# Loads of v and stores of x cut at other partitions in a talking-heads attention kernel

## The chip, the cores and the metric

The kernel runs on one core of one Trainium2 chip. The metric is the time of one execution on the device in microseconds (us). The kernel before takes 866.6 us, the median of three runs that lie between 863.59 and 868.46 us.

## What is computed

Four batches of attention with 12 heads, 448 positions and a head size of 64, with heads mixed before and after the softmax, and behind it a bilinear feed-forward layer. All inputs are float32. Cut to what matters:

```python
scores = scale * np.matmul(q, k.transpose(0, 1, 3, 2))
scores = np.einsum('bhij,hg->bgij', scores, w_pre)
attn = np.exp(scores - np.max(scores, axis=-1, keepdims=True))
attn = attn / (np.sum(attn, axis=-1, keepdims=True) + 1e-09)
attn = np.einsum('bhij,hg->bgij', attn, w_post)
out = np.matmul(attn, v)                       # [4, 12, 448, 64]
x = out.transpose(0, 2, 1, 3).reshape(1792, 768)
a, b = x @ w_a, x @ w_b                        # 768 x 1536 each
result = (a * b) @ w_out
```

## The kernel before

The attention fills roughly the first 350 us, the feed-forward layer the rest.

Positions are cut into chunks of 120, 120, 120 and 88 per batch, and each chunk into units of 20 positions (23 units a batch, 92 in all). The main loop takes one unit in each step `s`. On TensorE a step holds four pieces of work: `premix` of its unit (L345, tile `mp`), one `qk` (L281, tile `pst`, scores of one pair of heads for a later chunk), one `av` (L429, tile `xp`, attention times v for two heads of a group of six units that is finished) and `postmix` of the unit before (L391, tile `pp`).

Between `qk` and `premix` the scores are laid out anew: `gather` (L325, tile `sb<-s`) copies them from SBUF to SBUF with four transfers for each unit, issued by POOL. A unit's gathers are issued four steps ahead (`AH`) into tiles that rotate over five buffers.

All other transfers of this stage go through the queue of SP, which issues them in the order of the program: loads of q (L251) and k (L235), loads of v (`load_v`, L206 to L218), stores of x to a buffer in device memory (L439, `xd<-xs`), and two writes of 4 bytes in each step (L221, `paced`), which wait for a result of VectorE and so hold SP's queue to the pace of the computation. `plan_loads` chooses the step of each load of q, k and v by an estimate of what each step already carries; its estimates for v stand in a list `v_size`, which the change leaves alone.

Loads of q (from the chunk with number 3 on) and of k (from the second batch on) are already cut in two by partitions, at row 88 (`LOW`, `part`). `load_k` of the later batches puts its rows in a tile with two buffers (`kraw`), so that the load with number i + 2 waits until `order_k` (L242 to L244) has copied the load with number i away.

`load_v` brings the v of one batch in 14 pieces, 7 for each half of the heads. A half lies in a tile of 128 partitions by 6 heads by 4 by 64. Pieces 0 to 2 are partitions 0 to 63, two heads each; pieces 3 and 4 are partitions 64 to 111, three heads each; pieces 5 and 6 fill the rest. The first 8 pieces of the first batch are loaded before the main loop, the others from step 3 on, those of a later batch while the batch before is computed.

`av` fills the tile `xs` (128 partitions by 3 by up to 120 columns) twice for each group; its store is issued one step later (`later(..., 1)`). There are 32 stores of x: 24 of 180 KB and 8 of 132 KB, eight for each batch. They are read back after the attention stage (L523, `xhl<-xd`).

Of the kernel before, what the change touches and what calls it, by code (L numbers as in the profile page):

```python
# [22 lines left out]
def talking_heads_bilinear_kernel(  # L23
# [11 lines left out]
    nc = tc.nc  # L35
    B, _, G, S = k.shape
# [10 lines left out]
    R = 4  # L47
    P = S // R
    C = 64
    X = P - C  # L50
# [21 lines left out]
    V_PIECES = 14  # L72
    PACKET = 170
    LOW = 88
    OWN = 3
    SPREAD = 2
    RAW_AT = 74
# [8 lines left out]
    for b in range(B):  # L86
        t0 = 0
        while t0 < S:
            n = min(CHUNK, S - t0)
# [30 lines left out]
    xd = [dram.tile([128, KD, S], F32, name=f"xd{b}") for b in range(B)]  # L120
# [21 lines left out]
    def later(fn, n=3):  # L142
        todo_at.setdefault(now[0] + n, []).append(fn)
# [61 lines left out]
    def load_v(b, i):  # L205
        g, i = divmod(i, V_PIECES // 2)  # L206
        to, of = vt[b % 2][g], v[b, g]
        if i < 3:
            heads = slice(2 * i, 2 * i + 2)
            nc.sync.dma_start(out=to[:C, heads], in_=of[:C, heads])  # L210
        elif i < 5:
            heads = slice(3 * (i - 3), 3 * (i - 3) + 3)
            nc.sync.dma_start(out=to[C:P, heads, :R - 1], in_=of[C:, heads, :R - 1])
        elif i == 5:
            for j in range(R - 1):
                nc.sync.dma_start(out=to[P:, :, j], in_=of[C + Y * j:C + Y * j + Y, :, R - 1])
        else:
            nc.sync.dma_start(out=to[C:, :, R - 1], in_=of[:C, :, R - 1])  # L218
# [4 lines left out]
    def part(half):  # L223
        return slice(0, 128) if half is None else slice(LOW * half, LOW + (128 - LOW) * half)

# [191 lines left out]
    def av(a, p):  # L417
        b, u0, _ = groups[a]
        t0 = (u0 - b * NUB) * QU
        n = min(AVC, S - t0)  # L420
        g = p // 3
        if p % 3 == 0:
            xp = ps.tile([128, 512], F32, tag="m" if a == NA - 1 else "x", name="xp", bufs=3 if a == NA - 1 else 1)
            xps[g] = xp[:, :3 * AVC].rearrange("p (a t) -> p a t", a=3)
        xp = xps[g]
        for r in range(R):
            for e in range(2):
                h = 2 * p + e
                nc.tensor.matmul(  # L429
                    xp[64 * e:64 * e + 64, p % 3, :n],  # L430
                    lhsT=vt[b % 2][g][:, h % G, r],
                    rhs=ptt[a][:, r, h, :n],
                    start=(r == 0),
                    stop=(r == R - 1),
                )
        if p % 3 == 2:
            xs = x_p.tile([128, 3, AVC], F32, tag="xs", name="xs")
            nc.vector.tensor_copy(xs[:, :, :n], xp[:, :, :n])
            later(lambda: nc.sync.dma_start(out=xd[b][:, 3 * g:3 * g + 3, t0:t0 + n], in_=xs[:, :, :n]), 1)  # L439

    items, late, between, after, ready = {}, {}, {}, {}, {}
    starts = [u for u in range(NU) if units[u][1] == 0] + [NU]
# [2 lines left out]
    for c in range(1, NC):  # L445
        b, t0, _ = chunks[c]
# [11 lines left out]
    for a in range(NA):  # L458
        b, u0, n = groups[a]
        for p in range(H // 2):  # L460
            av_at[a, p] = u0 + n + (AV_AT if n == GU else AV_SHORT)[p]
            if a < NA - 1:
                items.setdefault(av_at[a, p], []).append((av, a, p))

    def plan_loads():
# [6 lines left out]
        def place(first, last, it, n, parts=(0,)):  # L472
            for x in parts:
                u = min(range(min(first, last), last + 1), key=lambda u: (busy[u], u if len(parts) > 1 else -u))
                busy[u] += n
                full = sum(1 for y in between.get(u, ()) if y[0] in (load_q, load_k, load_v))
                (after if full else between).setdefault(u, []).append(it + ((x,) if len(parts) > 1 else ()))
                first = u
# [23 lines left out]
        for b in range(1, B):  # L502
            first = max(av_at[per_b * (b - 2) + per_b - 1, H // 2 - 1] + 1 if b > 1 else 0, V_FIRST + V_PIECES - V_EARLY)
            for i in sorted(range(V_PIECES), key=lambda i: (i // 7, -v_size[i % 7])):
                place(first, av_at[per_b * b, i // 7 * 3] - V_LEAD, (load_v, b, i), v_size[i % 7])
# [346 lines left out]
    with tc.manual_schedule():  # L852
# [16 lines left out]
        for i in range(G):  # L869
            if i == 1:  # L870
                spread_q(0, 1, nc.vector)
                setup_w()
            if i + 4 < G:
                load_k(0, i + 4)
                order_k(0, i + 4, pool, pool)
            if i == 2:
                load_q(1, 0)
                load_q(1, 1)
                for j in range(V_EARLY):
                    load_v(0, j)  # L880
                load_q(2, 0)
            qk(0, i, 0)
# [15 lines left out]
        for s in range(NU + 2):  # L898
# [19 lines left out]
            for it in items.get(s, ()):  # L918
                if it[0] is qk:
                    it += (it[2] % OWN if s not in late else 1,)  # L920
                it[0](*it[1:])
# [15 lines left out]
        for p in range(6):  # L937
            av(NA - 1, p)
            if p == 2:
                for fn in split_all(2):  # L940
                    fn()
# [73 lines left out]
        for n in range(NP * 2):  # L1015
            i, r = divmod(n, R6)
# [59 lines left out]
```

## Time and profile before

| | |
|---|---|
| three runs | 863.59, 866.6, 868.46 us |
| the profiled execution | 864.87 us, of which its span 863.2 us |
| TensorE matmul busy | 838.9 us, 97% of the span |
| VectorE, ScalarE, POOL busy | 500.7, 414.1, 478.9 us |
| DMA packets | 105306, 165.90 MB |
| SP's queue (q1) and POOL's queue (q0) | 46.1% and 18.5% of the time of 16 DMA engines |
| granted TensorE clock, mean | 0.995 |

The busy time of TensorE says little about how near it is to its peak, since matmuls are pipelined and their ends are modelled. What tells more is the idle time of its own, its releasers, and the distance from one `premix` to the next, which is 3.45 us in a step that holds all four pieces of work.

### The profile page before, as it was taken

How to read it: one execution, taken by the hardware profiler on the slowest of the kernel's cores; microseconds unless marked ns; L12 is line 12 of the kernel's file. 1: busy time of each engine (PE TensorE's matmuls, PEld its weight loads, DVE VectorE, ACT ScalarE, POOL GpSimd, SP SyncE). 2: the span in 40 equal slices, each digit the busy share in tenths (PEclk: the TensorE clock that was granted, in tenths of full speed). 3: DMA queues.
4: the chain of work that ended last, by engine and by line, in shares of the span. 5: the costliest groups of instructions: out<-in, count | busy, mean ns of one | idle time of the engine just before them, and what ended most of it. 6: DMA issues, size and time to landing. Idle time of an engine off the chain costs nothing.

```text
span 863.2 us, 26217 instructions
## 1 busy us (share of the span) xinstructions
PE 838.9 (97%) x10612; PEld 675.4 (78%) x10612; DVE 500.7 (58%) x989; ACT 414.1 (48%) x864; POOL 478.9 (55%) x595
## 2 busy tenths in 40 slices
PE   7898999999999999999999999999999999999998
PEld 3455665666656656798999999999999998999997
DVE  4777778777787776455433433363446245655761
ACT  3676677677777777634323232322232145333330
POOL 6786777677767865026446533678657743222220
PEclk9999999999999999999999999999999999999999
DMA  7687777787979984764643634566565488655551
GB/s 195 176 197 181 190 191 204 181 201 190 201 169 203 217 200 110 218 203 163 190 145 134 217 134 158 185 222 247 198 221 193 156 314 301 214 209 190 205 198 65
DMA packets 105306, 165.90 MB, mean 192 GB/s; under 512 B 50014, under 2 KB 81114, under 8 KB 105186
## 3 DMA queue, kind: packets, MB, share of 16 engines
q1 hardware_dynamic: 76738, 126.11, 46.1%
q0 software_dynamic: 28448, 38.11, 18.5%
q8 instruction: 84, 1.38, 0.7%
q14 instruction: 36, 0.29, 0.1%
HBM read 84.16 MB, written 41.29 MB: 145 GB/s over the span
## 4 chain that ended last, share of the span: by engine, by line
PE 65%; DMA 10%; POOL 9%; issue 7%; DVE 5%; ACT 2%; SPq 1%; POOLq 0%; DVEq 0%; ACTq 0%
PE xp L429 8%; PE pp L391 7%; PE pst L281 7%; PE mp L345 6%; PE po L759 6%; PE po L760 6%; PE po L758 6%; PE pb L641 3%; PE pa L639 3%; PE pa L640 3%; PE pa L641 3%; PE pb L639 3%; PE pb L640 3%; DMA sb<-s 3%; DMA kraw<-in_k_dram 2%
## 5 line engine op out<-in xcount | busy, mean ns | idle before, releaser
L325 POOL DMA_DIRECT2D sb<-s x354 | 204.1, 588 | 66.2 <-PE mp L345 28.9
L358 ACT ACTIVATE a<-mp,nm 124x448 f32<-124x448 f32 x180 | 112.6, 631 | 57.8 <-DVE nm L355 57.7
L355 DVE TENSOR_REDUCE nm<-mp 124x1 f32<-124x448 f32 x180 | 104.2, 619 | 51.2 <-PE mp L345 48.5
L661 DVE TENSOR_TENSOR hf<-pb,sa 128x448 f32<-128x448 f32 x47 | 29.4, 625 | 170.0 <-PE pb L641 155.8
L429 PEld LDWEIGHTS xp<-pt,v 128*64 128x64 f32 x1536 | 74.1, 137 | 61.7 <-issue 44.7
L645 ACT COPY sa<-pa 128x448 f32<-128x448 f32 x47 | 25.0, 533 | 175.8 <-PE pa L641 175.8
L408 ACT COPY pt<-pp 128x480 f32<-128x480 f32 x176 | 91.2, 576 | 34.6 <-PE pp L391 33.5
L391 PE MATMUL pp<-kr,a 60*64 60x60 f32 x5040 | 99.3, 223 | 5.3 <-issue 4.9
L391 PEld LDWEIGHTS pp<-kr,a 60*64 60x64 f32 x5040 | 86.5, 135 | 21.9 <-issue 9.6
L641 PE MATMUL pb<-xhl,wl 128*128 128x448 f32 x282 | 102.4, 363 | 0.9 <-POOL wl L624 0.9
L639 PE MATMUL pb<-xhl,wh 128*128 128x448 f32 x282 | 102.3, 363 | 0.0
L640 PE MATMUL pb<-xhl,wh 128*128 128x448 f32 x282 | 102.3, 363 | 0.0
L281 PE MATMUL pst<-k,q 64*64 64x448 f32 (+1 forms) x728 | 92.5, 546 | 7.5 <-DVE s L306 4.4
L345 PE MATMUL mp<-sb,wp 60*64 60x448 f32 x720 | 96.2, 547 | 2.7 <-DMA sb<-s 1.8
L640 PE MATMUL pa<-xhl,wh 128*128 128x448 f32 x264 | 95.7, 363 | 0.0
L641 PE MATMUL pa<-xhl,wl 128*128 128x448 f32 x264 | 95.7, 363 | 0.0
L639 PE MATMUL pa<-xhl,wh 128*128 128x448 f32 x264 | 95.7, 363 | 0.0
L429 PE MATMUL xp<-pt,v 128*64 128x120 f32 (+1 forms) x1536 | 93.5, 266 | 0.8 <-ACT pt L408 0.8
L630 POOL TENSOR_TENSOR wl<-v,wh 128x768 fp32r<-128x768 f32 x21 | 39.2, 1868 | 98.9 <-ACT wh L629 96.4
L759 PE MATMUL po<-hhl,wh 128*128 128x448 f32 x252 | 91.6, 364 | 1.6 <-DVE hhl L717 1.6
L758 PE MATMUL po<-hhl,wh 128*128 128x448 f32 x252 | 91.4, 363 | 0.0
L760 PE MATMUL po<-hhl,wl 128*128 128x448 f32 x252 | 91.4, 363 | 0.0
(117 smaller groups left out, 1432.7 us busy)
## 6 DMA issues: line engine op xcount, KB each, us to landing
sb<-s POOLq DMA_DIRECT2D x350, 105.0 KB, 5.1
hhl<-hd SPq DMA_DIRECT2D x42, 448.0 KB
v<-in_w_ab_dram SPq DMA_DIRECT2D x22, 768.0 KB
hd<-hf SPq DMA_DIRECT2D x48, 224.0 KB
v<-in_w_out_dram SPq DMA_DIRECT2D x12, 768.0 KB
wod<-cw SPq DMA_DIRECT2D x21, 384.0 KB
v<-wod SPq DMA_DIRECT2D x21, 384.0 KB
xhl<-xd SPq DMA_DIRECT2D x24, 224.0 KB
```

What stands on the lines that cost most here:

```text
L281: nc.tensor.matmul(out[64 * e:64 * e + cols.stop - cols.start], lhsT=qt[c, i // QG][rows, i % QG, cols], rhs=kt[b, i][rows],)
L325: (nc.sync if ALONE <= u <= AH and i % 2 else nc.gpsimd).dma_start(out=sbt[u][i % 2][r:r + m * H], in_=rows)
L345: nc.tensor.matmul(mt[u, i // 2][col:col + M], lhsT=wp[r:r + m, :M], rhs=tiles[i % 2][r:r + m])
L358: nc.scalar.activation(a[:m], mp[:m], ACTF.Exp, bias=nm[:m], scale=1.0, accum_out=rss[u][:m, j:j + 1])
L391: nc.tensor.matmul(pp_t[i][C * e:C * e + C, H * r:H * r + H, j, :m], lhsT=at[u, j][rows, x:x + C], rhs=kr[rows, j, :, :m],)
L429: nc.tensor.matmul(xp[64 * e:64 * e + 64, p % 3, :n], lhsT=vt[b % 2][g][:, h % G, r], rhs=ptt[a][:, r, h, :n], start=(r == 0), stop=(r == ...
L639: nc.tensor.matmul(o, lhsT=hh[:, off + k], rhs=x[:, 0, k], start=first, stop=False)
L640: nc.tensor.matmul(o, lhsT=hh[:, off + k], rhs=x[:, 1, k], start=False, stop=False)
L641: nc.tensor.matmul(o, lhsT=ll[:, off + k], rhs=x[:, 0, k], start=False, stop=last)
L758: nc.tensor.matmul(po, lhsT=hh[:, k], rhs=t[:, 0, k], start=(k == 0), stop=False)
L759: nc.tensor.matmul(po, lhsT=hh[:, k], rhs=t[:, 1, k], start=False, stop=False)
L760: nc.tensor.matmul(po, lhsT=ll[:, k], rhs=t[:, 0, k], start=False, stop=(k == KH2 - 1))
```

## The change

Two things. In `load_v`, pieces 0 to 2 become partitions 0 to 23 with all six heads, and partitions 24 to 63 with three heads in each of two pieces; pieces 3 and 4 become partitions 64 to 87 and 88 to 111 with all six heads each. The number of pieces and their bytes in sum stay (600 KB for the five pieces of a half). In `av`, each store of x of the first three batches becomes two stores, of partitions 0 to 87 and 88 to 127, issued one behind the other in the step in which the one store was issued; the last batch keeps its eight stores whole.

```diff
+    C_LOW = 24
...
         if i < 3:
-            heads = slice(2 * i, 2 * i + 2)
-            nc.sync.dma_start(out=to[:C, heads], in_=of[:C, heads])
+            rows, heads = ((slice(0, C_LOW), slice(0, G)), (slice(C_LOW, C), slice(0, 3)), (slice(C_LOW, C), slice(3, G)))[i]
+            nc.sync.dma_start(out=to[rows, heads], in_=of[rows, heads])
         elif i < 5:
-            heads = slice(3 * (i - 3), 3 * (i - 3) + 3)
-            nc.sync.dma_start(out=to[C:P, heads, :R - 1], in_=of[C:, heads, :R - 1])
+            n = X // 2
+            rows = slice(C + n * (i - 3), C + n * (i - 3) + n)
+            nc.sync.dma_start(out=to[rows, :, :R - 1], in_=of[rows, :, :R - 1])
...
             nc.vector.tensor_copy(xs[:, :, :n], xp[:, :, :n])
-            later(lambda: nc.sync.dma_start(out=xd[b][:, 3 * g:3 * g + 3, t0:t0 + n], in_=xs[:, :, :n]), 1)
+            for half in range(2) if b < B - 1 else (None,):
+                rows = part(half)
+                later(lambda rows=rows: nc.sync.dma_start(out=xd[b][rows, 3 * g:3 * g + 3, t0:t0 + n], in_=xs[rows, :, :n]), 1)
```

## Rows read from the trace of the kernel before

**Rows 1.** The page, part 1: engine, busy us (share of the span), instructions.

```profile
PE 838.9 (97%) x10612; PEld 675.4 (78%) x10612; DVE 500.7 (58%) x989; ACT 414.1 (48%) x864; POOL 478.9 (55%) x595
```

**Rows 2.** Busy us (instructions) of each engine by stretch, then clock, DMA share, GB/s.

```profile
57.00:72.00 15.00, 11.85 (x305) 7.19 (x303) 10.52 (x32) 8.85 (x21) 10.65 (x19) 1.00 0.92 212
...
100.00:160.00 60.00, 60.00 (x1540) 36.84 (x1537) 48.30 (x118) 43.64 (x108) 45.12 (x85) 1.00 0.78 203
160.00:170.00 10.00, 8.57 (x193) 5.00 (x184) 6.42 (x20) 6.48 (x15) 4.43 (x10) 1.00 0.65 150
...
300.00:320.00 20.00, 17.63 (x440) 11.71 (x440) 12.99 (x32) 14.78 (x34) 14.41 (x28) 1.00 0.95 219
```

**Rows 3.** PE's waits, 15 to 70 us: waiting line <- releaser: us, times, longest.

```profile
PE mp L345 <- DMA sb<-s: 1.8, 2, 1.5
...
PE pp L391 <- issue: 0.9, 1, 0.9
```

**Rows 4.** PE's waits, 70 to 305 us.

```profile
PE pst L281 <- DVE s L306: 3.6, 2, 2.4
PE pp L391 <- issue: 2.1, 3, 1.4
```

**Rows 5.** PE's waits, 305 to 345 us.

```profile
PE pp L391 <- issue: 1.9, 2, 1.5
```

**Rows 6.** Chain of waits, 44 to 82 us: start us, us, what.

```profile
51.89 5.01 DMA kraw<-in_k_dram
...
57.59 5.35 DMA kraw<-in_k_dram
...
63.27 7.10 DMA kraw<-in_k_dram
```

**Rows 7.** Timeline of DVE, 60 to 75 us: start, us, line, out<-in [idle before <-releaser].

```profile
70.47 0.29 DVE L242 COPY k<-kraw 128x256 f32<-128x256 f32 x1 [2.94 <-DMA kraw<-in_k_dram]
```

**Rows 8.** Timeline of SP's queue, 44 to 82 us.

```profile
59.95 0.77 SPq L251 DMA_DIRECT2D qraw<-in_q_dram  x2
60.76 0.41 SPq L439 DMA_DIRECT2D xd<-xs  x1
61.28 0.41 SPq L221 DMA_DIRECT2D paced<-nm  x1
61.78 0.30 SPq L235 DMA_DIRECT2D kraw<-in_k_dram  x1
63.01 0.21 SPq L221 DMA_DIRECT2D paced<-rc  x1
63.27 0.29 SPq L235 DMA_DIRECT2D kraw<-in_k_dram  x1
```

**Rows 9.** One line's instructions, L439: ns min/median/max, first and last start.

```profile
L439 SPq DMA_DIRECT2D xd<-xs x32: 371/517/2732, 60.8 to 370.1; - x32
```

**Rows 10.** The same for L325, the gathers issued by POOL.

```profile
DMA to landing us min/median/max: 2.8/5.1/8.1
```

**Rows 11.** The page, part 3: the queue that carries instructions.

```profile
q8 instruction: 84, 1.38, 0.7%
```

**Rows 12.** DMA queues, 158 to 165.8 us: packets, MB, share of 16 engines.

```profile
q0 software_dynamic: 772, 1.07, 67.0%
q1 hardware_dynamic: 205, 0.26, 10.9%
q14 instruction: 1, 0.01, 0.2%
```

**Rows 13.** DMA queues, 165.8 to 170 us.

```profile
q8 instruction: 1, 0.02, 1.3%
```

**Rows 14.** Timeline of PE, 166 to 169 us.

```profile
168.33 0.27 PE L391 MATMUL pp<-kr,a 60*64 60x60 f32 x2 [1.43 <-issue]
```

## The prediction, made before the changed kernel ran

> **What bounds the kernel now.** I read the page first. TensorE's matmuls are busy 838.9 us of a span of 863.2 [rows 1], so about 24 us of idle time on TensorE is all that a change of transfers can give back; how much it can cost has no such limit. The table by stretch comes next, since an average over the span hides where those 24 us lie. From 100 to 160 us TensorE is busy for 60.00 of 60 us while the DMA engines are at 0.78 [rows 2]: in the steady part of the attention stage transfers are hidden, and nothing that makes one of them faster is seen. The places to look at are the stretches in which TensorE is not full: 57 to 72 (11.85 of 15), 160 to 170 (8.57 of 10) and 300 to 320 (17.63 of 20) [rows 2].
>
> What TensorE waits for in them I take from its waits, over 15 to 70, 70 to 305 and 305 to 345 us [rows 3, 4, 5]. Three kinds are within reach of transfers. First, 1.8 us for gathers at the start [rows 3]. Second, one wait of 2.4 us for a copy of scores on VectorE [rows 4], which the chain of waits follows back to loads of k: three landings in series, 5.01, 5.35 and 7.10 us long [rows 6], because a k load must find one of two buffers emptied by the copy before it; VectorE itself is idle for 2.94 us in front of the copy that needs the last one [rows 7]. That is a place where a landing is paid for in full. Third, the waits put down to "issue", 0.9, 2.1 and 1.9 us [rows 3, 4, 5]. For these I looked at the queues: 84 packets of the instruction queue [rows 11] stand against 2 x 10612 instructions of TensorE [rows 1], which is 253 instructions a packet. Between 158 and 165.8 us no such packet moves (the queue is absent there) [rows 12]; one moves after that [rows 13], and TensorE, which stood still for 1.43 us, starts again at 168.33 [rows 14]. I read this as TensorE running out of instructions because a block of them came late. It is a reading of one place, not proven for the other four.
>
> **The change part by part.** *Pieces of v.* Nothing is added: five pieces of seven keep their number and their sum of 600 KB (3 x 128 + 2 x 108 before, 144 + 2 x 120 + 2 x 108 after). Runs within a row get longer. They are due five steps ahead of their first use, about 17 us at 3.45 us a step, while the slowest gather landed in 8.1 us [rows 10], the nearest row for a landing in this stage. So on the path they cost 0; if the cover were gone, a piece would cost what it lands late, at most the difference between a slow and a middling landing, 8.1 - 5.1 = 3.0 us. Beside the first gathers, which are waited for, the same bytes move; between -1.8 (that wait gone) and +1.8 (doubled) I take 0, since the bytes are the same.
>
> *Stores of x.* Twenty-four stores become 48. Each further one takes SP between 0.30 us (a load of 88 rows of k, [rows 8]) and 0.52 us (the median store now, [rows 9]), so 7.2 to 12.5 us in all, spread over the steps from 60 to about 297 us. SP's queue carries only transfers, so what counts is who stands behind. Queued behind a store in its step are the two paced writes, and loads of q, k and v. The one place where that matters is the first store at 60.76 us: 0.41 us behind it stands a paced write and behind that, at 61.78, a part of a k load [rows 8], in the series that ends with the wait of 2.4 us. That part is issued 0.30 to 0.52 us later. The other part, at 63.27, follows a paced write at 63.01 that waits for VectorE; SP is free from 61.78 + 0.30 = 62.08, 0.93 us before, so this part is not issued later. The landing that the chain names is that of the part at 63.27, 7.10 us, against 5.01 and 5.35 for the two before it, which had no store of x just ahead of them [rows 6]. The difference, at most 2.1 us, is what a store ahead can be blamed for. So the bounds of the split store at this place are -2.1 (the interference disappears) and +2.1 (it doubles). I take +0.4: the bytes are the same, and the second part of the store starts one issue later, 0.41 us [rows 8], so the k load runs that much longer beside it.
>
> Here the Trainium skill speaks against the change. Its page "DMA: Bandwidth & Descriptors", section "Rules for kernel authors", says of two transfers to disjoint partition halves not to bother, since they use the same engines, and to use one transfer of 128 partitions. By it the part of +0.4 would lean to the upper bound of +2.1; no run here has shown that yet. The same page, section "Why a DMA increments its semaphore by 16 and not by 1", says that a transfer is spread over the largest number up to 16 that divides the sizes of its outer dimensions: 16 for 64, 48 or 128 partitions, 12 for 24, 11 for 88 and 10 for 40, on the lowest-numbered engines. By that rule the first ten engines would carry 12 rows of each store in place of 8, and four or five others would be left to the gathers and to instructions; no row here names an engine.
>
> *Instruction blocks.* If they wait behind other transfers, parts of other sizes move these waits. Changed transfers run up to 297 us, so of the three waits the 1.9 us after 305 cannot go [rows 5]; 0.9 + 2.1 = 3.0 us can [rows 3, 4]. Bounds: -3.0 (all in time) and +3.0 (twice as much). Where the block was late, POOL's gathers took 67.0% of the DMA engines' time and everything of SP 10.9% [rows 12], so SP's part of what stood in the way is 10.9 / 77.9 = 14%, and not all of it is v and x. 14% of 2.1 is 0.3; I take -0.3.
>
> *The sum* is 0 + 0 + 0.4 - 0.3 = +0.1 us. The profiled execution took 864.87 us, 1.7 under the median of the three runs, 866.6; I set the base at their middle, 865.7, and so forecast 865.8 us.
>
> **The rivals.** *Faster: instructions and first gathers come in time.* The late blocks before 305 us and the wait for the first gathers go: -3.0 - 1.8 = -4.8, so 865.7 - 4.8 = 860.9 us. For it: these waits end with a transfer or right behind one, and the stretch 57 to 72 has the DMA engines at 0.92 [rows 2]. Against it: the gathers, not SP, filled the engines where I could look. The skill's count of engines, named above, would be its mechanism.
>
> *Slower: the series of k loads.* In the second batch each landing is passed on to TensorE in full, as it already waits 2.4 us at the end. If the parts of x and v make the two shorter landings as long as the third, that is 7.10 - 5.01 + 7.10 - 5.35 = 3.8 us; if the same series in a later batch then reaches TensorE as well, with the 2.1 us by which the landings differ, 865.7 + 3.8 + 2.1 = 871.6 us. It decides from a landing of a k part above some 7 us. For it: the wait is there already. Against it: only one store lies within the first series, and in the steady stretch TensorE was full.
>
> *The change does nothing.* The same bytes go at the same moments, the DMA engines even it out: 865.7 us, inside the forecast.
>
> **How the numbers follow.** The smallest difference that a measurement of this kernel can tell from no change is about 0.5%, 4.3 us, here 862.3 and 870.9 around the median. The forecast of 865.8, with the bounds of its terms mostly offsetting one another, gets 0.50, no effect 0.14; both are within. The faster rival gets 0.20, the slower one 0.16. Adding the bounds of k and instructions gives 865.7 - 5.1 = 860.6 and + 5.1 = 870.8. The range is 860.5 to 870.5: it holds the forecast and most of the faster rival and leaves the slower one out.
>
> **What would show it.** L439 should have 56 instructions. Right: the wait of L281 for L306 near 72 us stays at 2.4 +- 0.5; issue waits between 70 and 305 us sum to 1 to 3 us; the steady steps stay at 3.45 us; nothing changes after 350 us. The k step is wrong if that wait is gone or doubled; the instruction step if its sum falls under 0.5 or rises above 4; the hidden v if `av` or its weight loads wait for a load of v. The forecast as a whole fails if the steady stretch is no longer full, since then a resource that I hold to be hidden has come to bound it.

## The result and the profile after

The changed kernel takes 871.59 us, the median of 20 runs, beside 867.33 us for 20 runs of the kernel before. The ratio is 1.0062, with a 95% interval of 1.0043 to 1.0082: slower, by about 5 us, and outside the forecast range of 860.5 to 870.5. The profiled execution took 873.36 us with a span of 871.6 us. It lies 1.8 us above its median and the one of before 2.5 us below, so the two traces differ by more, 8.4 us of span, than the kernels do. Of the 8.4 us, 6.9 are lost in the attention stage: the feed-forward matmul L639 into `pa` (L643 now) first starts at 394.5 us where it started at 387.6. Line numbers after the change are one or two higher (L281 is L283, L391 is L393, L439 is L443).

The table by stretch, with the columns of [rows 2]:

```profile
57.00:72.00 15.00, 13.90 (x352) 8.44 (x344) 11.71 (x33) 10.39 (x26) 11.08 (x21) 1.00 0.83 206
100.00:160.00 60.00, 57.17 (x1451) 35.50 (x1444) 44.05 (x108) 41.37 (x103) 41.30 (x78) 1.00 0.79 195
160.00:170.00 10.00, 10.00 (x247) 6.12 (x242) 8.85 (x26) 7.82 (x19) 6.98 (x13) 1.00 0.77 188
```

The stretch from 100 to 160 us, which was full before [rows 2], has lost 2.83 us of TensorE's time at nearly the same share of the DMA engines. The granted clock is the same. In part the loss has only moved, since the 10 us behind it, with 8.57 before, are now full. The waits of TensorE between 70 and 305 us answer to [rows 4]:

```profile
PE pp L393 <- issue: 4.2, 5, 1.7
PE pst L283 <- DVE s L308: 3.9, 4, 1.9
PE mp L347 <- issue: 2.2, 1, 2.2
PE pst L283 <- POOL q L266: 0.7, 1, 0.7
PE xp L431 <- issue: 0.6, 1, 0.6
PE pst L283 <- ACT s L310: 0.4, 1, 0.4
```

They sum to 12.0 us against 5.7. The issue waits alone, those for which the profile shows no releaser, went from 2.1 to 4.2 + 2.2 + 0.6 = 7.0 us. The other issue waits of before, 0.9 and 1.9 us [rows 3, 5], are gone, so from 0 to 350 us they rose by 2.1 only, from 4.9 to 7.0, and all waits of TensorE there from 17.1 to 21.9. Before 70 us the wait for the first gathers grew, to be compared with [rows 3]:

```profile
PE mp L347 <- DMA sb<-s: 3.1, 3, 1.2
```

The longest issue wait is one place in the timeline of TensorE, to be compared with [rows 14], and the DMA queues in the 5.6 us before it, from 116.6 to 122.2 us, answer to [rows 12]:

```profile
125.18 0.59 PE L347 MATMUL mp<-sb,wp 60*64 60x448 f32 x2 [2.18 <-issue]
```

```profile
q0 software_dynamic: 488, 0.69, 54.2%
q1 hardware_dynamic: 980, 0.40, 40.1%
q14 instruction: 1, 0.01, 0.9%
```

Again there is no packet on the instruction queue (q8) in the stretch before the wait, as in [rows 12]; here SP's queue held 40.1% of the engines' time where it was 10.9%. From 122.2 to 125.3 us, a stretch that holds the wait, there is one:

```profile
q8 instruction: 1, 0.02, 2.1%
```

It lands 1.8 us before TensorE starts again. This settles what the prediction left as the reading of one place: of the issue waits over 0.2 us between 15 and 350 us, in the traces of all kernels here, each of the 144 ends 1.2 to 2.2 us behind the landing of an instruction packet. Of the 300 other waits of TensorE, 16% end that near behind one.

The series of k loads no longer stands in the chain of waits as three landings: only the last is left. SP's timeline around the first store, answering to [rows 8], the chain of waits [rows 6], and the copy on VectorE that waits for the last load [rows 7]:

```profile
61.62 0.87 SPq L443 DMA_DIRECT2D xd<-xs  x2
...
62.92 0.48 SPq L237 DMA_DIRECT2D kraw<-in_k_dram  x1
...
64.48 0.54 SPq L237 DMA_DIRECT2D kraw<-in_k_dram  x1
```

```profile
64.48 6.20 DMA kraw<-in_k_dram
```

```profile
70.77 0.29 DVE L244 COPY k<-kraw 128x256 f32<-128x256 f32 x1 [2.38 <-DMA kraw<-in_k_dram]
```

The k part landed in 6.20 us, where it took 7.10, and VectorE's idle time in front of the copy is 2.38 us, where it was 2.94. TensorE's wait behind it, from 60 to 80 us, is 1.4 us, where it was the 2.4 of [rows 4]:

```profile
PE pst L283 <- DVE s L308: 1.4, 1, 1.4
```

The store line has 56 instructions, as it should, and a median of 494 ns (its row stands beside [rows 9]):

```profile
L443 SPq DMA_DIRECT2D xd<-xs x56: 286/494/1448, 61.6 to 376.8; - x56
```

What the prediction had not looked at is who else waits. The waits of POOL between 60 and 305 us, before and after, then those of SP's queue:

```profile
POOL sb L325 <- PE mp L345: 26.2, 24, 3.5
POOL q L264 <- DMA qraw<-in_q_dram: 9.3, 5, 3.0
```

```profile
POOL q L266 <- DMA qraw<-in_q_dram: 26.6, 8, 5.0
...
POOL sb L327 <- PE mp L347: 13.5, 12, 2.4
```

```profile
SPq L221 <- DMA v<-in_v_dram: 4.6, 9, 0.9
SPq L235 <- DMA kraw<-in_k_dram: 3.1, 1, 3.1
```

```profile
SPq L223 <- DMA v<-in_v_dram: 6.4, 7, 1.6
SPq L237 <- DMA kraw<-in_k_dram: 6.1, 3, 2.5
...
SPq L223 <- DMA xd<-xs: 2.5, 4, 1.5
```

POOL waits for loads of q for 26.6 us in place of 9.3. It used to wait for TensorE to free the gathers' buffers, which is to be ahead; now it waits for data, and the gathers stand behind the copy of q in its order. L223 is a paced write. It needs a value of VectorE and nothing of v, yet SP waits in it for loads of v to land. In the instruction records SP's transfers name eight semaphores in turn (all 402 of the first 350 us before the change), and SP waits for the earlier transfer on a semaphore before it issues the next. That is the counter meant below and in the expectations. All waits of SP for transfers sum to 21.8 us (30 waits) before and 29.2 us (44 waits) after.

### The profile page after: what moved, and what is told of

Its sections match the earlier page's. It is cut to its first block, busy times and chain, and to the rows that moved or that the text cites. A ratio compares the mean times of both kernels' runs of the same rounds, so it can differ in the third digit from the quotient of the medians.

```text
span 871.6 us, 26239 instructions
## 1 busy us (share of the span) xinstructions
PE 842.4 (97%) x10612; PEld 674.4 (77%) x10612; DVE 500.6 (57%) x989; ACT 414.1 (48%) x864; POOL 478.9 (55%) x595
## 4 chain that ended last, share of the span: by engine, by line
PE 81%; DMA 8%; DVE 3%; POOL 2%; issue 2%; ACT 1%; SPq 0%; DVEq 0%; POOLq 0%
PE xp L431 8%; PE pp L393 7%; PE pst L283 6%; PE pb L645 6%; PE pa L643 6%; PE pa L645 6%; PE pa L644 6%; PE pb L643 6%; PE pb L644 6%; PE mp L347 6%; PE po L763 6%; PE po L764 6%; PE po L762 6%; DMA sb<-s 5%; POOL sb L327 2%
## 5 line engine op out<-in xcount | busy, mean ns | idle before, releaser
L410 ACT COPY pt<-pp 128x480 f32<-128x480 f32 x176 | 91.1, 575 | 35.2 <-PE pp L393 34.4
L347 PE MATMUL mp<-sb,wp 60*64 60x448 f32 x720 | 98.3, 549 | 5.4 <-DMA sb<-s 3.1
L393 PE MATMUL pp<-kr,a 60*64 60x60 f32 x5040 | 98.3, 222 | 5.0 <-issue 4.2
L393 PEld LDWEIGHTS pp<-kr,a 60*64 60x64 f32 x5040 | 85.6, 134 | 21.9 <-issue 10.5
L643 PE MATMUL pb<-xhl,wh 128*128 128x448 f32 x282 | 102.2, 362 | 0.0
L283 PE MATMUL pst<-k,q 64*64 64x448 f32 (+2 forms) x728 | 92.5, 547 | 9.1 <-DVE s L308 5.0
L643 PE MATMUL pa<-xhl,wh 128*128 128x448 f32 x264 | 95.7, 362 | 0.0
```

Of the source, the lines that this page charges most:

```text
L283: nc.tensor.matmul(out[64 * e:64 * e + cols.stop - cols.start], lhsT=qt[c, i // QG][rows, i % QG, cols], rhs=kt[b, i][rows],)
L347: nc.tensor.matmul(mt[u, i // 2][col:col + M], lhsT=wp[r:r + m, :M], rhs=tiles[i % 2][r:r + m])
L393: nc.tensor.matmul(pp_t[i][C * e:C * e + C, H * r:H * r + H, j, :m], lhsT=at[u, j][rows, x:x + C], rhs=kr[rows, j, :, :m],)
L643: nc.tensor.matmul(o, lhsT=hh[:, off + k], rhs=x[:, 0, k], start=first, stop=False)
```

## The experiments

Eighteen kernels ran, each in 12 timed runs beside 23 to 35 runs of the kernel before on the same chip. The table has the ratio to the kernel before, the change in the number of SP's transfers, and two sums from the waits between 60 and 305 us in the profiled execution: SP's waits for transfers, and all waits of POOL in its copies of q. The last column sums TensorE's issue waits from 0 to 350 us. These sums are of one execution each, which can lie far from the median of its kernel: that of x_64 is the fastest of its 12, 4.9 us below their median, that of x_merged lies 5.7 below. Theories have letters: by P the row counts of the parts make the loss, by N the number of transfers; by Q a stand of SP's queue makes it, so that fewer transfers help; L keeps a loss of v of its own beside that.

| kernel | ratio (95% interval) | transfers | SP | POOL, q | issue |
|---|---|---|---|---|---|
| before | 1 | 0 | 21.8 | 15.6 | 4.9 |
| the change | 1.0062 (1.0043 to 1.0082) | +24 | 29.2 | 31.9 | 7.0 |
| v_only | 1.0016 (0.9989 to 1.0044) | 0 | 19.5 | 23.4 | 8.3 |
| v_012 | 1.0012 (0.9983 to 1.0041) | 0 | 20.0 | 20.2 | 5.2 |
| v_32 | 1.0039 (1.0013 to 1.0066) | 0 | 18.7 | 28.2 | 10.7 |
| v_short | 1.0025 (0.9997 to 1.0052) | 0 | 27.0 | 26.0 | 9.1 |
| v_whole | 1.0081 (1.0053 to 1.0108) | -24 | 9.5 | 23.7 | 11.8 |
| x_only | 1.0036 (1.0010 to 1.0063) | +24 | 35.2 | 29.2 | 4.3 |
| x_64 | 1.0062 (1.0038 to 1.0086) | +24 | 28.8 | 38.7 | 2.6 |
| x_extra | 1.0023 (0.9999 to 1.0047) | +24 | 28.8 | 24.8 | 5.5 |
| x_unpaced | 1.0028 (1.0002 to 1.0055) | 0 | 32.9 | 27.9 | 2.5 |
| qk_whole | 0.9940 (0.9911 to 0.9968) | -44 | 11.6 | 2.7 | 7.2 |
| k_whole | 0.9961 (0.9935 to 0.9987) | -18 | 25.0 | 23.3 | 5.8 |
| q_whole | 0.9950 (0.9924 to 0.9977) | -26 | 14.5 | 6.1 | 2.9 |
| x_qk_whole | 0.9959 (0.9923 to 0.9996) | -20 | 12.5 | 3.6 | 5.7 |
| v_qk_whole | 0.9971 (0.9940 to 1.0001) | -44 | 12.4 | 3.7 | 5.5 |
| all_qk_whole | 0.9942 (0.9918 to 0.9966) | -20 | 5.9 | 4.6 | 4.4 |
| all_q_whole | 1.0026 (0.9992 to 1.0060) | -2 | 11.8 | 7.9 | 4.6 |
| all_k_whole | 1.0024 (0.9993 to 1.0054) | +6 | 32.7 | 28.0 | 8.5 |
| x_merged | 1.0018 (0.9981 to 1.0054) | -56 | 9.2 | 3.2 | 2.5 |

**One half of the change at a time, and two cuts at other rows.** Both halves alone are the change with the other half taken back.

> The new pieces of v alone, the stores of x whole. Base 867.3 us before, ratio of the whole change 1.0062, that is 5.4 us. Theory P (the row counts of the parts make the loss: transfers cut at rows 24, 40 and 88 crowd together, and instruction blocks of TensorE come late): v and x carry 600 x 8 = 4800 KB and 24 stores of 4032 KB, so v should bring about half, a ratio of 1.003, and PE's waits put to issue between 70 and 305 us should lie between the 2.1 us of before and the 7.0 us of the change (4.2 + 2.2 + 0.6). Theory N (the number of stores makes it: 24 further transfers in SP's queue): no loss here, 1.000. Theory L (the longer runs of the v pieces, which hold a DMA engine for longer at a time): all of the loss here, 1.006.

> The stores of x of the first three batches cut at row 88 alone, v as before. Theory P: about half of the loss, 1.003, with issue waits between 2.1 and 7.0 us. Theory N: all of it, 1.006. Theory L: none, 1.000.

```diff
 (x_64)
-                rows = part(half)
+                rows = slice(0, 128) if half is None else slice(64 * half, 64 * half + 64)
```

> The stores of x of the first three batches cut at row 64, so the same 24 further transfers as with row 88, v as before. Theory P: no loss, 1.000, issue waits near 2.1 us, since 64 rows spread as evenly as 128. Theory N: all of the loss, 1.006, as with row 88. Theory L: 1.000.

```diff
 (v_32, with C_LOW = 32 and the stores of before)
-            n = X // 2
-            rows = slice(C + n * (i - 3), C + n * (i - 3) + n)
+            rows = (slice(C, C + 16), slice(C + 16, P))[i - 3]
```

> The pieces of v in parts of 32 partitions with six heads and 32 partitions with three heads twice, and of 16 and 32 partitions in place of 48 and 48: as many transfers and the same long runs as in the change (6 KB and 3 KB), stores of x whole. Theory P: no loss, 1.000. Theory N: 1.000. Theory L: 1.006, as the new pieces of v alone.

Measured: 1.0016, 1.0036, 1.0062 and 1.0039. The stores alone lose, and their cut at row 64 loses no less than that at row 88; the 32-row pieces of v lose no less than the 24- and 40-row ones, whose own loss is not clear of 0. Theory P, that the row counts make the loss, falls. By the Trainium skill, "DMA: Bandwidth & Descriptors", section "Why a DMA increments its semaphore by 16 and not by 1", parts of 64, 32 and 16 rows use 16 engines and those of 88, 40 and 24 use 11, 10 and 12; the runs show no gain from the former. The losses of the two halves, 0.0016 and 0.0036, add up to 0.0052 beside 0.0062 for the whole.

**Number of transfers, with no more bytes or with no more transfers.**

```diff
 (x_extra: stores whole)
+            if b < B - 1:
+                e0 = 2 * a + g
+                later(lambda: nc.sync.dma_start(out=extra[e0:e0 + 1], in_=xs[:1, 0, :1]), 1)
```

> Stores of x whole, as before, but behind each of the 24 stores of the first three batches one further write of 4 bytes in SP's queue. Theory N (the number of transfers in SP's queue makes the loss, as each takes one of the eight completion counters that the profile shows SP's transfers to share, and SP stands still until the transfer before it on that counter has landed): a loss like that of the cut stores, 1.003 to 1.006, and SP's waits for transfers between 60 and 305 us above the 21.8 us of before, near 29 to 35 us as with the cut stores. Rival B (the same bytes in two parts is what costs, by their order on the DMA engines): 1.000, SP's waits near 22 us.

```diff
 (x_unpaced: stores cut at row 88)
-            if j0 == 0:
+            if j0 == 0 and u not in store_at:
                 pace(2 * u + 1, rc[:, :1])
```

> Stores of x of the first three batches cut at row 88, and in the steps in which they are issued the second paced write of 4 bytes left out, so SP issues as many transfers as before. It leaves the writes of 4 bytes out; the output is computed in full. Theory N: the loss goes, 1.000, and SP's waits for transfers fall back towards 22 us from 35. Rival B: 1.003 to 1.004 as with the cut alone.

Measured: 1.0023, with an interval that just holds 1, and 1.0028. The second is a miss for theory N: with the number of transfers as before, the loss stayed, and so did SP's waits (32.9 us). So the count alone is not the measure. The paced write that was left out also holds SP's queue to the computation, so this kernel changes the pace as well. In x_extra SP's waits rose to 28.8 us, as theory N had it; whether the 24 small writes cost time stays inconclusive.

**The same cut taken back on other loads.** Loads of q and k are cut at row 88 in the kernel before as well.

```diff
 (qk_whole; k_whole has the first edit alone, q_whole the second)
-        rows = part(half)
-        nc.sync.dma_start(out=kraw[b, i][rows], in_=k[b, rows, i])
+        if not half:
+            nc.sync.dma_start(out=kraw[b, i], in_=k[b, :, i])
...
-        rows, sl = part(half), slice(G * t0 + QG * j * n, G * t0 + QG * (j + 1) * n)
-        nc.sync.dma_start(out=qraw[c, j][rows], in_=q[b, rows, sl].rearrange("d (h t) -> d h t", h=QG))
+            sl = slice(G * t0 + QG * j * n, G * t0 + QG * (j + 1) * n)
+            nc.sync.dma_start(out=qraw[c, j], in_=q[b, :, sl].rearrange("d (h t) -> d h t", h=QG))
```

> The kernel before with loads of q and k whole in place of two parts cut at row 88: 44 transfers fewer in SP's queue, the same bytes. Theory N: faster, by the measure of 24 transfers for 0.3 to 0.6% some 0.5 to 1%, 0.990 to 0.995, with fewer waits of SP for transfers. Rival B: also faster. Theory P (rows 88 and 40 crowd the transfers): faster as well. Theory S (the cut lets the parts be spread over steps, which is worth more than their number costs): slower, 1.003 or more.

> The kernel before with only the loads of k whole (18 transfers fewer). Whole q and k came to 0.994. Theory Q: the waits of scores behind VectorE's copies of k go (3.6 us between 70 and 305 us before), while POOL's waits for q stay near 15 us: 0.996 to 0.998.

> The kernel before with only the loads of q whole (26 transfers fewer). Theory Q: POOL's waits in front of spread_q fall from 15.6 us to a few, SP's waits for transfers from 21.8 to about 15 us: 0.996 to 0.998. If only the k half or only the q half of whole q and k makes its gain, one of these two runs is at 1.000 and the other at 0.994.

Measured: 0.9940, 0.9961 and 0.9950. Taking a cut back gains about what the change's cut loses, and each load has its part in it; the two alone sum to 0.0089 of gain beside 0.0060 together. In k_whole the wait of VectorE for k is all but gone while POOL still waits for q, and not for the 15 us expected but for 23.3. VectorE's waits for k, 60 to 305 us, before and in k_whole:

```profile
DVE k L242 <- DMA kraw<-in_k_dram: 4.9, 4, 2.9
```

```profile
DVE k L242 <- DMA kraw<-in_k_dram: 0.2, 1, 0.2
```

In qk_whole POOL's waits in its copies of q are down to this row:

```profile
POOL q L264 <- DMA qraw<-in_q_dram: 2.7, 2, 2.0
```

These edits do a second thing. A whole load is issued where its first part was, and the second part used to come later. In the trace of before the two parts of a q load from the main loop's plan are issued 3.7 us apart in the median (24 of 26 over 1 us), those of k 1.5 us. One q load from 100 us on, in SP's timeline of before and of q_whole:

```profile
101.08 0.30 SPq L251 DMA_DIRECT2D qraw<-in_q_dram  x1
...
104.51 0.29 SPq L251 DMA_DIRECT2D qraw<-in_q_dram  x1
```

```profile
100.81 0.36 SPq L251 DMA_DIRECT2D qraw<-in_q_dram  x1
```

So the gain can come from fewer transfers or from rows 88 to 127 being asked for earlier. A kernel with both parts at the place of the first was not run.

**The change on a queue with slack.** Each half of the change, then the whole of it, with q and k whole, or one of them.

> The stores of x cut at row 88 as in the change, v as before, and the loads of q and k whole. Whole q and k alone came to 0.994, the cut stores alone to 1.0036. Theory Q (the cut stores cost because SP stands longer for earlier long transfers and so the halves of q and k behind them come late to POOL and VectorE): with 44 transfers fewer in the queue there is slack, and the cut costs little: 0.994 to 0.996, POOL's waits in front of spread_q stay near the 2.7 us of whole q and k instead of 28 to 39. Rival A (the loss adds up, whatever else is in the queue): 0.9976 or more.

> The new pieces of v, stores of x whole, loads of q and k whole. The new pieces alone came to 1.0016 (32-row ones to 1.0039). Theory L (long runs of v hold a DMA engine, and instruction blocks come late): it is no matter of SP's queue, so the loss stays, 0.996 to 0.998, with issue waits of TensorE above the 7.2 us of whole q and k in all. Theory Q for v too: 0.994.

> The whole change (parts of v and of x) with the loads of q and k whole. Whole q and k alone came to 0.994, with the cut stores 0.9959, with the new pieces of v 0.9971, the change alone to 1.0062. Theories Q and L together: the loss by x mostly gone, that by v kept: 0.996 to 0.999. Rival A (all adds up): 1.000 or more.

> The whole change with only the loads of q whole. The change alone came to 1.0062, with q and k whole to 0.9942, and whole q alone to 0.995. If the loss passes through the two parts of each q load (they come late to POOL, which issues the gathers behind them): as without the change, 0.995 to 0.997, POOL's waits for q a few us. If it passes through k: 0.999 to 1.001.

> The whole change with only the loads of k whole. Whole k alone came to 0.9961. If the loss passes through q: it stays, 1.000 to 1.003, with POOL's waits for q near the 32 us of the change. If it passes through k: 0.996 to 0.998.

Measured: 0.9959, 0.9971 and 0.9942 with both whole; 1.0026 with q and 1.0024 with k whole alone. With both whole, the entire change costs nothing that can be measured: 0.9942 beside 0.9940, with intervals of some 0.3% either way. That is the test that decides against rival A, which had 1.000 or more. For theory L it decides little: v_qk_whole came out at the 0.9971 that L had forecast, with an interval that begins at 0.9940, and the whole change, 0.9942, below the 0.996 to 0.999 of L but with an interval that reaches 0.9966. Waits of TensorE from 70 to 305 us, and POOL's for q from 60 to 305 us, in all_qk_whole:

```profile
PE pp L393 <- issue: 2.8, 4, 1.3
```

```profile
POOL q L266 <- DMA qraw<-in_q_dram: 4.6, 3, 2.0
```

All waits for scores (`pst`) are gone from TensorE there, and 12.0 us have become 2.8. One load whole was not enough, which I had expected of one of them: the loss does not pass through q alone, nor through k alone. From q_whole to all_q_whole it is 1.0026 - 0.9950 = 0.0076, from k_whole to all_k_whole 0.0063, both as large as without. In all_q_whole POOL waits little for q (7.9 us), and the time is lost nonetheless; there VectorE waits for k, 60 to 305 us, as it does in the change (5.6 us):

```profile
DVE k L244 <- DMA kraw<-in_k_dram: 7.2, 5, 3.9
```

In all_k_whole it is the other way round, with 28.0 us of POOL for q and 0.3 of VectorE for k.

**Run length, and larger transfers.**

```diff
 (v_012)
 pieces 0 to 2 as in the change, pieces 3 and 4 as before
 (v_short, in place of heads)
+            rs = (slice(0, 1), slice(1, 2), slice(2, R))[i]
+            nc.sync.dma_start(out=to[:C, :, rs], in_=of[:C, :, rs])
 (v_whole)
+        if i == 0:
+            nc.sync.dma_start(out=to[:C], in_=of[:C])
+        elif i == 3:
+            nc.sync.dma_start(out=to[C:P, :, :R - 1], in_=of[C:, :, :R - 1])
```

> Only pieces 0 to 2 of v in their new parts (24 and 40 partitions, runs of 6 KB and 3 KB in place of 2 KB), pieces 3 and 4 and the stores of x as before. Theory L (long runs hold a DMA engine, so instruction blocks and parts of q come late): the loss of the new pieces of v as a whole, 1.002 to 1.004, with issue waits of TensorE above the 4.9 us of before in all. If pieces 3 and 4 make it (their runs stay 768 bytes, but come from 24 rows with 18 runs in place of 48 rows with 9): 1.000.

> The kernel before with pieces 0 to 2 of v cut along r in place of heads: all six heads of 64 partitions, one r, one r and two r, so runs of 256 and 512 bytes in place of 2 KB, as many transfers and bytes. Theory L (the length of the runs is what makes instruction blocks late): not slower than before, 0.997 to 1.001, with issue waits of TensorE at or under the 4.9 us of before. Rival G (any other order of the v transfers than that of before is worse here, by size or by place): slower, 1.002 to 1.004.

> The kernel before with pieces 0 to 2 of v as one transfer of 64 partitions and six heads (384 KB, runs of 6 KB) and pieces 3 and 4 as one (216 KB): 24 transfers fewer, the same bytes, long runs. If fewer transfers help wherever they are (theory Q in its wide form): faster, 0.995 to 0.998. Theory L: slower, 1.002 to 1.004, with late instruction blocks where these pieces move.

Measured: 1.0012, 1.0025 and 1.0081. Between runs of 256 and 512 bytes and runs of 3 and 6 KB no difference shows; the interval of v_012 and that of v_short hold 1. One piece of 384 KB in place of three (and one of 216 KB in place of two) is the slowest kernel of all, beyond what either theory had forecast, though SP stands least of the kernels with q cut in two (9.5 us). It also moves the bytes of three steps in one, so that size and crowding are not told apart. Here the issue waits are plain, TensorE, 70 to 305 us:

```profile
PE pp L391 <- issue: 9.3, 8, 2.2
```

So theory Q in its wide form, fewer transfers are better wherever they are, falls too.

```diff
 (x_merged, on qk_whole)
+            if g == 0:
+                xss[a] = x_p.tile([128, 6, AVC], F32, tag="xs", name="xs", bufs=1)
+            xs = xss[a]
+            nc.vector.tensor_copy(xs[:, 3 * g:3 * g + 3, :n], xp[:, :, :n])
...
+            elif g == 1:
+                later(lambda: nc.sync.dma_start(out=xd[b][:, :, t0:t0 + n], in_=xs[:, :, :n]), 1)
```

> Loads of q and k whole, and one store of x for all six blocks of heads of a group in place of two of three for the first three batches (12 stores in place of 24, the second half's step). Meant as a version that beats both kernels. Theory Q: 0.990 to 0.994, as fewer long transfers stand in the queue; rival (a store of 360 KB is in flight for longer and holds up what stands behind it): 0.996 or more.

Measured: 1.0018, so the gain of whole q and k is gone. Not only the size of the store changed: the larger tile has one buffer (`bufs=1`) in place of two, so VectorE cannot fill it before the store ahead has landed. Its trace, of an execution among its fastest (span 860.7 us), has this wait of VectorE from 60 to 305 us, which before and qk_whole do not have:

```profile
DVE xs L440 <- DMA xd<-xs: 6.4, 2, 4.7
```

What stores of 360 KB cost by themselves is thus not shown. The version that beats both kernels is qk_whole, 861.66 us in the median beside 865.68.

## Why the prediction was wrong

**The failing step is the one on the stores of x.** It put them at +0.4 us, paid at one place, and at nothing in the rest of the stage. That what counts is who stands behind a store in SP's queue fits the runs; that the first store at 60.76 us is the one place where it matters does not. The cut stores alone cost 0.36% (x_only) and 0.62% (x_64), about 3 and 5 us, and in x_only TensorE does not wait for scores near 72 us at all, while its waits for scores from 70 to 305 us sum to 6.6 us, where they were 3.6.

The ground for it was the stretch from 100 to 160 us, taken for proof that transfers are hidden there. They were hidden by a margin that the view does not show. In this stretch POOL's waits for q went from 1.0 to 3.8 us and SP's for transfers from 2.3 to 7.6, and TensorE came to 57.17 of 60 us. In this trace 2.7 of the 2.83 us are issue waits, so it does not tie the loss to the stores by itself; the kernels do. The same stretch in x_only and x_64, then in x_qk_whole and all_qk_whole:

```profile
100.00:160.00 60.00, 58.32 (x1472) 35.60 (x1472) 45.35 (x116) 42.26 (x105) 44.58 (x84) 1.00 0.87 205
```

```profile
100.00:160.00 60.00, 57.03 (x1436) 34.84 (x1425) 43.76 (x113) 40.74 (x100) 43.75 (x83) 1.00 0.88 205
```

```profile
100.00:160.00 60.00, 60.00 (x1502) 36.77 (x1501) 50.35 (x121) 43.58 (x108) 45.31 (x85) 1.00 0.79 203
```

```profile
100.00:160.00 60.00, 59.63 (x1488) 36.84 (x1484) 48.66 (x118) 43.26 (x107) 45.11 (x84) 1.00 0.82 206
```

With the stores cut and nothing else the stretch is no longer full, and with q and k whole it is full again, or nearly. It is not the whole account either, since k_whole is faster than before with 58.90 us there. The prediction named a steady stretch that is no longer full as the sign on which the whole forecast fails.

**The base was too low.** It was set at 865.7 us, and 20 runs of the kernel before have a median of 867.33. Of the 5.8 us between the forecast and 871.59 this is 1.6; the rest is the change, forecast at +0.1 us and measured at 4.3 by the medians.

**The k step was right in its bounds and not in its sign.** Forecast was +0.4 us at the first series and a wait of TensorE there of 2.4 +- 0.5 us. The landing became shorter by 0.9 us, the idle time in front of the copy by 0.6 and the wait by 1.0, in one execution each. The part at 63.27 was said not to be issued later against the paced write before it; it kept its place right behind that write. The slower rival gave 871.6 us, which the measured 871.59 hits by its figure alone: its mechanism, landings of the first series above 7 us, did not come. That is luck.

**The pieces of v were put at 0 because they are due five steps ahead.** That holds for them: no wait for a load of v is among TensorE's waits. What they do to transfers around them was left out. In four forms with the same number of transfers the ratio was 1.0012 to 1.0039, and only that of v_32 is clear of 1. The cost of the form in the change is thus about 0 to 0.4% (v_only, up to 1.0044), and not settled more closely.

**Instruction blocks were mis-sized in the trace.** The term was -0.3 us with bounds of 3.0 either way; the issue waits from 70 to 305 us went up by 4.9, out of the bounds. From 0 to 350 us they went up by 2.1, so they are not most of the 8.4 us. The term rested on SP's part of 14% in the transfers ahead of one late block; ahead of the longest wait after, SP's part is 40.1 of 94.3%, or 43%. That these waits are for instructions is shown; that they are the cause of the loss is not: in the table they do not follow the ratio (7.2 us in qk_whole at 0.9940, 2.6 us in x_64 at 1.0062, though the trace of x_64 is of its fastest execution). In x_64 it is POOL that waits, for q, 60 to 305 us:

```profile
POOL q L264 <- DMA qraw<-in_q_dram: 26.8, 9, 5.6
```

**Halves or whole.** The rule to use one transfer of 128 partitions in place of two on disjoint halves (the Trainium skill, "DMA: Bandwidth & Descriptors", "Rules for kernel authors") agrees with the runs at both places tried, cut stores (1.0036 and 1.0062) and q and k made whole (0.9940), though the whole loads were also issued earlier. I had let it lean one landing by 2.1 us; it should have carried a rival about the whole stage. The count of engines, which I held to be the mechanism of the faster rival, showed no effect that these runs can tell.

**What stays open.** Shown is that the change costs 0.6% while q and k are cut in two, that the cut stores have a loss of their own, and that no cost is left that these runs can tell while q and k are whole. Not shown is what in whole loads takes it away, their smaller number or their earlier issue. Argued, not shown, is the way between: SP stands longer at its semaphores, loads behind it come late, POOL's gathers and the instruction blocks meet on crowded DMA engines. SP's waits do not follow the ratio throughout: v_32 loses with 18.7 us of them, under the 21.8 of before, and k_whole gains with 25.0. POOL's waits for q go with the ratio in most kernels, but k_whole is fast with 23.3 us of them, and v_whole, x_merged and all_q_whole are slower than theirs would tell. Their traces show other waits, for instructions, for the buffer of the store and for k, and no run tests these as causes.

## What to carry to other kernels

A stretch in which TensorE is full has a margin, and it has to be read from the waits of the engines that feed it before anything is costed at nothing. Where a queue already stands for its own transfers, cutting more of them in two is not free, and the first thing to try is to take existing cuts back. The last stall in a trace tells where time was paid, not what used it up: kernels that undo one part of the change did more for that here. Such an edit has to be checked for what else it moves, as here the time of issue or the number of buffers.

## What was not expected of the hardware

TensorE stood for its instructions in every profile, for 2.5 to 11.8 us in the first 350 us, with the longest single wait 3.23 us in v_32. All 144 of these waits over 0.2 us end 1.2 to 2.2 us after an instruction packet has landed. From the timeline of v_32:

```profile
132.40 0.86 PE L392 MATMUL pp<-kr,a 60*64 60x60 f32 x43 [3.23 <-issue]
```

And how rows are shared out among parts, 88 and 40 or 64 and 64, or whether a run is 256 bytes or 6 KB long, made no difference that these runs can tell, while 384 KB in one piece and one step cost 0.8%.
